# Block 0's first product, summed unit by unit in shared PSUM banks, with a new order of the whole program

## The chip, the cores and the metric

The kernel runs on one core of a Trainium2 chip. The metric is the device time of one execution in microseconds; the median of three runs of the kernel before is 976.9 us (976.35 to 977.07). A core has TensorE (PE, matrix products, with its weight loads PEld), VectorE (DVE), ScalarE (ACT), GpSimd (POOL) and SyncE (SP, which here only starts transfers). TensorE writes to PSUM, eight banks of 128 partitions x 512 fp32 values; VectorE and ScalarE read PSUM. Lines are quoted as L and a number; "before" and "now" numbers differ by up to 42, since the file grew.

## The reference

Random-feature attention, then a two-layer network on its output; the shapes are 8 batches, 8 heads, 576 positions, 64 columns, 128 features; 4608 tokens of width 512, hidden width 2048.

```python
def phi(x):                                  # x: q or k, scaled by 64 ** -0.25
    proj = einsum('bhsd,md->bhsm', x, omega)
    h = proj - sum(x * x, -1) / 2
    return exp(h - max(h, -1)) / sqrt(m)
kv = einsum('bhsm,bhsd->bhmd', k_p, v);  z = sum(k_p, axis=2)
num = einsum('bhsm,bhmd->bhsd', q_p, kv)
den = einsum('bhsm,bhm->bhs', q_p, z)[..., None] + 1e-06
x = (num / den).transpose(0, 2, 1, 3).reshape(4608, 512)
out = gelu(x @ w_in) @ w_out
```

The two weights arrive as 64-bit floats and are converted on the chip.

## The kernel before

**Work.** A *unit* is a pair of heads of one batch: 32 units, four to a batch (j = 0 to 3). The four units of a batch give the four 128-row slices of x, so a product x @ w_in over 512 columns is a sum of four pieces, one per unit. Units 0 to 7 are computed in plain fp32: projections (`pair`, L657, and `shared`, L664), maxima and shifts on VectorE (`top` L669, `shift_tiles` L678), exponentials on ScalarE (L673, L682), the sums over keys (`kv`, L689), transposes of q (`q_trans`, L727), numerators and denominators (`num_plain`, L737), reciprocals (`rcp`, L763 on) and the division into x (`div`, L800), each of the last in two halves. The later units use split numbers (`proj` L902, `proj_q` L924, `kv_split` L1003, `num` L746).

**Blocks.** The network runs over 13 blocks of tokens: 128, eleven times 384, 256. Block 0 uses the converted fp32 weights (`mm1` L1176, `gelu` L1187, `mm2` L1202). All others use weights and activations split in two fp16 parts, with three products for one: `mm1` (L1181) adds 12 products into a bank, `gelu` (L1189), `g_high` (L1193) and `g_low` (L1197) make the two parts, `mm2` adds three products (L1205 to L1207). The weights are converted in 16 pieces (`w_hi` L426, `w_lo` L435, `w_rmax` L438, `w_shift` L442, `w_round` L453), scaled by a maximum over all of them (`wchain_b` L503 and on), and then split (`w_high` L485 on ScalarE, `w_low` L489 on VectorE), 16 column blocks for each of w_in and w_out.

**Banks.** PSUM's eight banks form three rings: `at` with three buffers, `acc` with three, and `h` with two (`hb0`, `hb1`). The units of batch 0 may use all three rings, later units only `at`. Block 0's first product takes one `h` bank for each of 16 column blocks of 128.

**Order.** A planner (`Planner.run`) takes all operations with their costs and dependencies and lists them in time: on each engine it picks, among those that can start, the one with the earliest due time. Due times come from tables: `FIRST` gives a fixed sequence to the operations that it names, `STARTS` the blocks, `UDUE` the units' divisions, `OFF` a shift by kind of operation. The program is written in the order of that list, every engine runs its own part strictly in that order, and semaphores hold the dependencies. Where the planner sees TensorE without work, between `wk0` and `wk` microseconds of its own clock, it puts in `fill`: four products of the identity (L381) into columns of `hb0` that nobody reads.

## Time and profile before

| | |
|---|---|
| median of three runs | 976.9 us |
| profiled execution: device time | 975.53 us |
| its span, first to last instruction | 973.8 us |
| TensorE / weight loads busy | 963.4 / 602.3 us |
| VectorE / ScalarE / GpSimd busy | 715.4 / 730.0 / 350.4 us |
| identity products (L381) | 312, 21.8 us |
| block 0's first product (L1176) | 64 products, 17.4 us |
| granted TensorE clock | 1.00 |

A group row names line, engine, operation, tiles and shapes, the count, then busy time and the mean of one in ns (products overlap, so busy time over count is less than the mean), then idle time ahead of it and what ended that. An fp32 product leaves two records, an fp16, bf16 or rounded fp32 one leaves one. A timeline row has start, duration, engine, line, operation and count of equal instructions in a row; a bracket tells of idle time before it. The row of a stretch has busy time and instruction count of each engine, then granted clock, share of the transfer engines and GB/s.

### The profile page before, as it was taken

What the parts mean: (1) busy time and instruction counts of PE and PEld (TensorE: products, weight loads), DVE (VectorE), ACT (ScalarE), POOL (GpSimd) and SP (SyncE); (2) the same over time, 40 slices, a digit from 0 to 9 for tenths busy, and PEclk for the clock granted to TensorE, in tenths of its full rate; (3) what the DMA queues carried; (4) which work ended last, traced back from release to release, by engine and by line L of the source; (5) the groups of instructions that cost most, each with busy time, mean ns of one, the idle gap of its engine ahead of it and who ended that gap; (6) DMA issues with size and microseconds to landing.
All of it is one profiled execution on the core that took longest, in us unless ns stands there. A gap on an engine that the chain in (4) does not pass through costs nothing.

```text
span 973.8 us, 18152 instructions
## 1 busy us (share of the span) xinstructions
PE 963.4 (99%) x6324; PEld 602.3 (62%) x6324; DVE 715.4 (73%) x1948; ACT 730.0 (75%) x1504; POOL 350.4 (36%) x560
## 2 busy tenths in 40 slices
PE   8999999999999999999999999999999999999998
PEld 7777665665566666666565665566656656555576
DVE  5899899977888889878797888777767778621111
ACT  6979897887689879787798878877776986643243
POOL 2444334742166264353255335245216522200000
PEclk9999999999999999999999999999999999999999
DMA  8756123321041041031221132022003200000000
GB/s 305 229 182 227 70 73 134 98 82 55 1 118 61 26 139 47 25 91 45 75 82 49 30 127 66 14 72 61 24 33 86 62 23 12 1 33 1 1 34 22
DMA packets 39083, 70.96 MB, mean 73 GB/s; under 512 B 5712, under 2 KB 14288, under 8 KB 38992
## 3 DMA queue, kind: packets, MB, share of 16 engines
q1 hardware_dynamic: 38992, 69.81, 23.1%
q8 instruction: 50, 0.82, 0.4%
q14 instruction: 41, 0.34, 0.1%
HBM read 60.36 MB, written 9.44 MB: 72 GB/s over the span
## 4 chain that ended last, share of the span: by engine, by line
PE 96%; DVE 2%; DMA 1%; ACT 0%; issue 0%; SPq 0%; ACTq 0%; DVEq 0%
PE hb L1181 37%; PE acc L1205 12%; PE acc L1207 12%; PE acc L1206 12%; PE at L746 4%; PE at L924 3%; PE at L902 3%; PE at L1003 2%; PE hb L381 2%; PE hb L1176 2%; PE acc L1202 1%; PE at L657 1%; PE at L737 1%; PE at L689 1%; PE hb L689 1%; PE at L727 1%
## 5 line engine op out<-in xcount | busy, mean ns | idle before, releaser
L1181 PE MATMUL hb<-xh,wih 128*128 128x384 f16 (+1 forms) x768 | 247.2, 322 | 0.6 <-DVE gl L1197 0.4
L1181 PE MATMUL hb<-xl,wih 128*128 128x384 f16 (+1 forms) x768 | 247.2, 322 | 0.0
L1181 PE MATMUL hb<-xh,wil 128*128 128x384 f16 (+1 forms) x768 | 247.1, 322 | 0.0
L894 POOL TENSOR_TENSOR r<-xt,r 64x256 fp32r<-64x256 f32 (+2 forms) x216 | 171.8, 814 | 202.7 <-ACT r L889 161.3
L1205 PE MATMUL acc<-woh,gh 128*128 128x512 f16 (+1 forms) x560 | 211.4, 377 | 0.0
L1207 PE MATMUL acc<-wol,gh 128*128 128x512 f16 (+1 forms) x560 | 210.5, 376 | 0.0
L1206 PE MATMUL acc<-woh,gl 128*128 128x512 f16 (+1 forms) x560 | 210.5, 376 | 0.0
L1197 DVE SCALAR_TENSOR_TENSOR gl<-hb,bs,gh 128x384 f16<-128x384 f32 (+1 forms) x192 | 115.2, 600 | 126.0 <-ACT gh L1193 124.2
L1181 PEld LDWEIGHTS <-wih 128*128 128x128 f16 x1536 | 147.0, 98 | 95.2 <-issue 1.7
L1189 ACT ACTIVATE hb<-hb,bs 128x384 f32<-128x384 f32 (+1 forms) x192 | 104.5, 545 | 86.8 <-PE hb L1181 84.5
L1193 ACT ACTIVATE gh<-hb,bs 128x384 f16<-128x384 f32 (+1 forms) x192 | 109.2, 569 | 51.5 <-PE acc L1207 35.5
L1181 PEld LDWEIGHTS <-wil 128*128 128x128 f16 x768 | 75.1, 98 | 50.2 <-issue 1.6
L889 ACT CAST r<-xt 128x256 fp32r<-128x256 f32 (+2 forms) x216 | 81.5, 403 | 25.8 <-PE at L902 10.5
L1207 PEld LDWEIGHTS <-gh 128*128 128x128 f16 x576 | 56.4, 98 | 64.5
L1205 PEld LDWEIGHTS <-gh 128*128 128x128 f16 x576 | 56.1, 97 | 47.4 <-issue 0.4
L1206 PEld LDWEIGHTS <-gl 128*128 128x128 f16 x576 | 56.5, 98 | 42.1
L803 DVE TENSOR_TENSOR w<-at,rt 64x128 f32<-64x128 f32 (+6 forms) x168 | 54.7, 325 | 4.3 <-DVE rt L770 0.5
L757 ACT ACTIVATE dt<-at,vsc 64x288 f32<-64x288 f32 x96 | 47.6, 495 | 5.2 <-PE at L746 3.0
L902 PE MATMUL at<-om,r 128*128 128x256 f32 x216 | 50.3, 325 | 0.2
L924 PE MATMUL at<-r,om 128*128 128x288 f32 x192 | 50.4, 351 | 0.0
L906 ACT COPY lo<-at 128x256 f32<-128x256 f32 (+1 forms) x120 | 40.4, 349 | 2.2 <-PE at L902 1.5
L963 DVE TENSOR_TENSOR ql<-qt,qh 128x576 fp32r<-128x576 f32 x48 | 37.3, 782 | 6.1 <-ACT qh L960 6.0
(218 smaller groups left out, 1690.6 us busy)
## 6 DMA issues: line engine op xcount, KB each, us to landing
xt<-in_kT SPq DMA_DIRECT2D x56, 288.0 KB, 3.8
xt<-in_qT SPq DMA_DIRECT2D x56, 288.0 KB, 3.6
out_x<-o SPq DMA_DIRECT2D x35, 256.0 KB, 2.1
raw<-in_w_in SPq DMA_DIRECT2D x16, 512.0 KB, 5.2
raw<-in_w_out SPq DMA_DIRECT2D x16, 512.0 KB, 4.6
w<-in_v SPq DMA_DIRECT2D x6, 1280.0 KB, 6.1
wol<-in_v SPq DMA_DIRECT2D x6, 320.0 KB, 5.9
vt<-in_v SPq DMA_DIRECT2D x2, 320.0 KB, 4.1
```

Source lines behind the costliest of these rows:

```text
L803: nc.vector.tensor_tensor(x[r, c0:c1], ps[r, r0:r1], rt[r, r0:r1], op=ALU.mult)
L889: nc.scalar.copy(G['r', u, x][:, 0:b - a], xf[:, a:b])
L894: nc.gpsimd.tensor_tensor(r, xf[D:, a:b], r, op=ALU.subtract)
L902: nc.tensor.matmul(o[:, t], r[:, t * P:(t + 1) * P], om, start=True, stop=True)
L924: nc.tensor.matmul(G['pp', u, NK + g][:, 0:HS], om[:, i], xr_part(u, NK + g), start=(i == 0), stop=(i == 1))
L1181: nc.tensor.matmul(h[:, 0:t], w, (G['xh', n, j], G['xh', n, j], G['xl', n, j])[k][:, 0:t], start=(i == 0), stop=(i == 3 * NJ - 1))
L1189: nc.scalar.activation(h, h, AF.Gelu, scale=G['bs', n][:, 2:3])
L1193: nc.scalar.activation(G['gh', n, c][:, 0:t], G['h', n, c][:, 0:t], AF.Copy, scale=G['bs', n][:, 3:4])
L1197: nc.vector.scalar_tensor_tensor(G['gl', n, c][:, 0:t], G['h', n, c][:, 0:t], G['bs', n][:, 3:4], G['gh', n, c][:, 0:t], op0=ALU.mult, op1 ...
L1205: nc.tensor.matmul(acc, gh[:, s], woh[:, c, c0:c1], start=(c == 0), stop=False)
L1206: nc.tensor.matmul(acc, gl[:, s], woh[:, c, c0:c1], start=False, stop=False)
L1207: nc.tensor.matmul(acc, gh[:, s], wol[:, c, c0:c1], start=False, stop=(c == NF - 1))
```

## The change

Block 0's first product takes one `h` bank for three column blocks (`HG = 3`; columns 0 to 383 of the bank, side by side; the sixteenth block is alone in the sixth). Each of the 64 products is an operation of its own (`mm1_early`) that depends on its column block's weights and its unit's x alone, so the slice of unit 0 can be added before unit 1 is done. Only the first product into a bank carries the start flag. `gelu` reads its third of a bank once all twelve products of that bank are in. `fill` no longer carries the start flag, since sums may be open in the same bank. `fill` ends at 60 us of the planner's clock in place of 100. All tables of the planner are new. The code for `nd2` is there, but `nd2` is 0, so `den` and `rcp` are as before.

```diff
-X = dict(fb=793.51, fbp=-272.45, fb0=327.13, fbb=-89.81, ..., wk=100.0, wk0=5.0, nd=1, sr=0, pmx=0, m0=5)
+X = dict(fb=739.58, fbp=-521.51, fb0=-190.76, fbb=289.99, ..., wk=60.0, wk0=5.0, nd=1, sr=0, pmx=0, m0=5, nd2=0, e0=1)
-FIRST = (1, 3, 0, 2, 6, 7, 8, 40, 4, 5, 42, 110, 76, 144, 41, ...
+FIRST = (1, 3, 6, 7, 2, 0, 40, 41, 142, 151, 4, 157, 5, 8, 10, ...
...
+    HG = 3
...
     def fill():
         for i in range(4):
-            nc.tensor.matmul(hb[0][:, T:], iz[:, 0:P], iz[:, P:], start=True, stop=True)
+            nc.tensor.matmul(hb[0][:, T:], iz[:, 0:P], iz[:, P:], start=False, stop=True, skip_group_check=True)
...
+    def hcols(c):
+        return G['h', 0, c // HG * HG][:, c % HG * TB[0]:(c % HG + 1) * TB[0]]
+
+    def mm1_early(c, j):
+        nc.tensor.matmul(hcols(c), wi32[:, c, j], xs(0, j)[:, 0:TB[0]], start=(c % HG == 0 and j == 0), stop=(j == NJ - 1), skip_group_check=True)
+
     def gelu(n, c):
         t = TB[n]
+        if n < N32 and X['e0']:
+            nc.scalar.activation(G['g', n, c][:, 0:t], hcols(c), AF.Gelu)
+            return
...
         if n < N32:
             xr = [xs_place(n, j)[1] for j in range(NJ)]
+            if X['e0']:
+                if c % HG == 0:
+                    key = ('h', n, c)
+                    cs = range(c, min(c + HG, NF))
+                    for j in range(NJ):
+                        for x in cs:
+                            op('PE', t * 4 / 2400 + .02, mm1_early, x, j, r=[('w32', 1, x), xr[j]], w=[key] if (x, j) != (c, 0) else [],
+                               new=[] if (x, j) != (c, 0) else [('h', key)], due=when(n, x + j / 4), kind='P')
+                op('ACT', 0.1 + t / 1000, gelu, n, c, r=[('h', n, c // HG * HG)], new=[('g', ('g', n, c))], tab='g', kind=k)
+                return
```

Three places of the built order. First TensorE, where the first pieces of block 0's first product stand now (L1210); before, L1176 first stands behind the first maximum of the weights. The other rows are the attention of units 1 to 3: projections (L670, L677), transposes (L740), key sums (L702) and unit 1's first numerator (L750); `hb_84` and `hb_85` are the two `h` banks, `w_71` the converted weights.

```order
L670 MATMUL at<-om_66,xt 128x128
L670 MATMUL acc<-om_66,xt 128x128
L740 MATMUL acc<-ident,w_71 128x128 x4
L1210 MATMUL hb_84<-xa,w_71 128x128
L702 MATMUL acc<-vt_73,et 128x65 x8
L702 MATMUL acc<-vt_73,et 128x130
L1210 MATMUL hb_85<-xa,w_71 128x128
L740 MATMUL at<-ident,w_71 128x128 x5
L1210 MATMUL hb_84<-xa,w_71 128x128
L677 MATMUL at<-om_66,xt 64x128 x4
L670 MATMUL acc<-om_66,xt 128x128 x8
L750 MATMUL acc<-w_71 64x288 x2
```

Three of the 18 products that now stand ahead of the first maximum are among these rows; two more stand just ahead and one just behind. In the old order none stands there.

Then TensorE at the mark that the prediction uses, the second numerator of unit 4. Before (the first row is unit 4's first numerator, the last two are the first of 16 equal pairs of identity rows, and the second numerator, L737, comes right behind those):

```order
L737 MATMUL at<-qh,kvz 64x288 x4
L1176 MATMUL hb_85<-xa,w_71 128x128 x4
L1176 MATMUL hb_84<-xa,w_71 128x128 x4
L1202 MATMUL acc<-w_71,g 128x512
L1176 MATMUL hb_85<-xa,w_71 128x128 x4
L657 MATMUL at<-om_66,xt 128x128 x8
L1176 MATMUL hb_84<-xa,w_71 128x128 x4
L1202 MATMUL acc<-w_71,g 128x512
L381 LDWEIGHTS ident
L381 MATMUL hb_84<-ident 128x128
```

Now (the last row is the second numerator):

```order
L670 MATMUL at<-om_66,xt 128x128 x8
L677 MATMUL at<-om_66,xt 64x128 x4
L1210 MATMUL hb_85<-xa,w_71 128x128 x8
L750 MATMUL at<-qh,kvz 64x288 x4
L1234 MATMUL acc<-w_71,g 128x512 x2
L1210 MATMUL hb_85<-xa,w_71 128x128 x3
L670 MATMUL at<-om_66,xt 128x128 x8
L1210 MATMUL hb_85<-xa,w_71 128x128
L750 MATMUL at<-qh,kvz 64x288 x4
```

Before, 16 identities stand between the second product (L1202) and that numerator; now unit 5's projections (L670) and one product of block 0 (L1210) stand directly ahead of it, and the identities are gone.

Last ScalarE, at block 1's first two activations (L1189 and its rounding L1193; L1221 and L1225 now). L485 (L498 now) are the splits of w_in (`wih`) and w_out (`woh`). Before:

```order
L711 ACTIVATE zr<-kvz 128x2
L485 ACTIVATE wih<-w_71,wsc 128x4x128 x5
L1189 ACTIVATE hb_85<-hb_85,bs 128x384
L1193 ACTIVATE gh<-hb_85,bs 128x384
L1212 COPY o<-acc 128x512
L1189 ACTIVATE hb_84<-hb_84,bs 128x384
L1193 ACTIVATE gh<-hb_84,bs 128x384
L485 ACTIVATE woh<-w_71,wsc 128x512 x4
```

Now:

```order
L498 ACTIVATE wih<-w_71,wsc 128x4x128
L744 COPY qh<-at 128x512
L498 ACTIVATE woh<-w_71,wsc 128x512 x5
L1221 ACTIVATE hb_85<-hb_85,bs 128x384
L1225 ACTIVATE gh<-hb_85,bs 128x384
L498 ACTIVATE woh<-w_71,wsc 128x512 x6
L1221 ACTIVATE hb_84<-hb_84,bs 128x384
L1225 ACTIVATE gh<-hb_84,bs 128x384
```

Ahead of the second rounding stand eleven more splits now, all of w_out: five ahead of the first activation and six behind it.

## The prediction

> **What bounds the kernel now.** I read the page first: busy shares, the forty slices, the chain that ended last.

> ```profile
> PE 963.4 (99%) x6324; PEld 602.3 (62%) x6324; DVE 715.4 (73%) x1948; ACT 730.0 (75%) x1504; POOL 350.4 (36%) x560
> DVE  5899899977888889878797888777767778621111
> PEclk9999999999999999999999999999999999999999
> PE 96%; DVE 2%; DMA 1%; ACT 0%; issue 0%; SPq 0%; ACTq 0%; DVEq 0%
> ```

> TensorE is busy for 963.4 of 973.8 us, and 96% of the chain is TensorE. Without the identity products every product is needed, so time can only come from the 10.4 us in which TensorE idles and from the identity products. VectorE is at 7 to 9 tenths for three quarters of the span: not the bound on average, perhaps in a stage. Next the groups of TensorE by line, which show the products that the change touches.

> ```profile
> L381 PE MATMUL hb<-ident 128*128 128x128 bf16 x312 | 21.8, 219 | 2.0 <-DVE w L698 0.6 <-DVE nm L669 0.5 <-ACT g L1187 0.4
> L1176 PE MATMUL hb<-xa,w 128*128 128x128 f32 x128 | 17.4, 281 | 0.0
> ```

> The 312 identity products (L381) cost 21.8 us, 0.070 us each; nothing reads them. Block 0's first product is 64 products in two records each, 17.4 us, 0.27 us per product. Then busy time by stretches, all engines, and below it that of the identity products alone.

> ```profile
> 20.00:30.00 10.00, 8.90 (x113) 7.21 (x112) 6.88 (x18) 8.89 (x26) 5.98 (x5) 1.00 0.86 262
> 40.00:50.00 10.00, 10.00 (x116) 7.62 (x113) 9.69 (x25) 9.60 (x28) 3.87 (x4) 1.00 0.70 231
> 60.00:70.00 10.00, 8.91 (x97) 7.39 (x97) 9.15 (x24) 7.03 (x11) 4.29 (x2) 1.00 0.63 201
> 80.00:90.00 10.00, 10.00 (x67) 7.33 (x63) 9.33 (x17) 9.47 (x13) 3.70 (x2) 1.00 0.58 209
> 120.00:140.00 20.00, 20.00 (x144) 12.78 (x143) 18.77 (x43) 18.93 (x33) 5.28 (x9) 1.00 0.24 69
> 140.00:180.00 40.00, 39.91 (x232) 22.66 (x231) 37.71 (x116) 32.14 (x75) 21.30 (x38) 1.00 0.40 126
> 700.00:800.00 100.00, 100.00 (x606) 59.66 (x605) 74.93 (x220) 80.86 (x169) 43.03 (x77) 1.00 0.15 44
> ...
> 20.00:30.00 10.00, 3.67 (x48) 2.93 (x48) 1.00 0.86 262
> 40.00:50.00 10.00, 2.91 (x40) 2.40 (x40) 1.00 0.70 231
> 60.00:70.00 10.00, 2.83 (x40) 2.63 (x41) 1.00 0.63 201
> 90.00:110.00 20.00, 0.39 (x4) 0.31 (x4) 1.00 0.46 162
> ```

> The columns after the stretch are TensorE, its weight loads, VectorE, ScalarE, GpSimd. A full TensorE before 70 us is an illusion: three tenths are identity products. From 80 us on there is nearly none, and TensorE stays full until the last stores. VectorE is at 9.69 of 10 at 40 to 50 and at 18.77 of 20 at 120 to 140. So the first 80 us are set by VectorE (and ScalarE, 9.60 at 40 to 50), with TensorE waiting under a cover of identities; afterwards TensorE sets the end with VectorE close behind. The time of the whole is the useful TensorE work that gets done in the first part.

> **The change, part by part.** *Identities.* The built program has 228 in place of 312: 84 x 0.070 = 5.9 us less. That isn't a gain yet: where TensorE would have waited anyway, an identity costs nothing, and its absence leaves a bare wait. The last of them now stand ahead of the first maximum of the weights (L503; L516 now), so no wait behind it has a cover.

> *The early products.* Their number and shapes are the same: cost 0. What moves is their place: 18 of the 64 now run before that maximum, where there were none; they need only the units done so far and the converted weights. They go into time that identities covered, so they are free where they lie and are worth 0.27 us each later. What counts is how much remains at a place whose time another engine sets.

> *The mark.* I take the second numerator of unit 4 (L737; L750 now), since there the trace shows who sets the time.

> ```profile
> 75.85 1.16 PE L657 MATMUL at<-om,xt 64*128 64x128 f32 x16
> 76.94 1.16 PE L1176 MATMUL hb<-xa,w 128*128 128x128 f32 x8
> 77.93 1.02 PE L1202 MATMUL acc<-w,g 128*128 128x512 f32 x2
> 78.79 1.06 PE L381 MATMUL hb<-ident 128*128 128x128 bf16 x16
> 79.78 1.19 PE L737 MATMUL at<-qh,kvz 128*64 128x288 f32 x8
> ...
> 77.04 1.29 DVE L669 TENSOR_REDUCE nm<-at 128x4 f32<-128x512 f32 x2 [0.61 <-PE at L657]
> 78.24 1.28 DVE L678 TENSOR_TENSOR et<-at,nm 128x512 f32<-128x512 f32 x2
> ```

> Unit 4's numerator needs `at` banks that unit 5's projections hold until VectorE has shifted them (L678, ends at 79.52); TensorE fills with 16 identities and starts at 79.78. VectorE sets this time. I counted both orders up to the mark. Every kind of product stands there in the same number (96 projections, 45 products of keys and values, two of block 0's second product and so on), except two: 304 identities against 228, and 24 of block 0's first products against 36. So at the mark the changed kernel has 12 x 0.27 = **3.3 us** more useful work behind it. VectorE has, from the end of unit 3's first half (L800, 61.77) to the mark, the same instructions but for one more weight split (L489), and one small reduction (L500) less.

> ```profile
> 61.25 0.52 DVE L800 TENSOR_TENSOR xa<-hb,rt 128x128 f32<-128x128 f32 x2
> 61.69 0.15 DVE L500 TENSOR_REDUCE wcm<-wmax 128x1 f32<-128x8 f32 x1
> L489 DVE SCALAR_TENSOR_TENSOR wil<-w,wsc,wih 128x512 f16<-128x512 f32 x13 | 9.4, 745 | 0.0
> ```

> That is 0.745 - 0.15 = **0.6 us** later, if unit 3 is ready when it was. The gain at the mark is 3.3 - 0.6 = 2.7. Behind it the old order has eight more identities, 8 x 0.070 = **0.6 us**, and the new one none. Sum: -3.3 us; 5.9 us of identities go, 2.6 us come back as bare waits, mostly ahead of this mark.

> *Where unit 3 is ready.* I take the old time. Bounds from both sides: the new order does the shared projections (L664) of units 0 and 1 together at the start, which answers VectorE's longest early wait, 3.0 us; that is the most I give it. Against it, omega is loaded after two of the inputs instead of before them, 0.58 + 0.43 us of issue, so all may start 1.0 us later; yet TensorE's own first wait, 1.96 us for an input, can shrink by as much.

> ```profile
> DVE nm L669 <- PE acc L664: 3.0, 2, 2.6
> 2.00 0.58 SPq L642 DMA_DIRECT2D xt<-in_kT  x1
> 2.63 0.43 SPq L642 DMA_DIRECT2D xt<-in_qT  x1
> 8.66 0.37 PE L657 MATMUL at<-om,xt 64*128 64x128 f32 x1 [1.96 <-DMA xt<-in_kT]
> ```

> *After the mark.* The new order puts more weight splits ahead of block 1's first activations: 27 in place of 16 ahead of the second rounding (L1193; L1225 now). Their cover is ScalarE's waiting.

> ```profile
> 120.88 0.58 ACT L1193 ACTIVATE gh<-hb,bs 128x384 f16<-128x384 f32 x1
> 121.36 2.55 ACT L485 ACTIVATE woh<-w,wsc 128x512 f16<-128x512 f32 x4
> 121.49 0.62 DVE L1197 SCALAR_TENSOR_TENSOR gl<-hb,bs,gh 128x384 f16<-128x384 f32 x1 [0.18 <-ACT gh L1193]
> 123.85 0.33 PE L1181 MATMUL hb<-xh,wih 128*128 128x384 f16 x1
> ACT g L1187 <- PE hb L381: 2.2, 1, 2.2
> ACT hb L1189 <- PE hb L1181: 1.9, 2, 1.4
> ACT g L1187 <- PE hb L1176: 1.8, 4, 0.7
> ```

> Eleven splits at 2.55 / 4 = 0.64 are 7.0 us; between 60 and 121 us ScalarE waited 2.2 + 1.9 + 1.8 us for TensorE, which is now earlier, and some 1.2 in smaller waits. I take 0, as nearly all of it is covered; the other end is a rival below. It and the early 3.0 us stand on opposite sides, and I let them cancel. The later blocks, 140 us on, have the same products in another order; TensorE was full there and I take 0, with 0.5 us either way (of the 40 us from 140 it idled 0.09).

> *Sum.* The profiled execution: span 973.8 - 3.3 = 970.5. Its device time was 975.53, and the median of the three runs is 976.9; the same 3.3 off the median gives **973.6 us**.

> **Rivals.** (1) *The front is released too.* VectorE's early 3.0 us wait goes and nothing eats it later: 973.6 - 3.0 = 970.6. For it: VectorE has 6.88 of 10 at 20 to 30. Against: it is full from 40, and ScalarE has no room either.

> (2) *The waiting only loses its cover.* VectorE sets not just the mark but everything up to 140 us; TensorE, 3 us ahead, runs into it again and the lead goes in waits for banks: 976.9 - 0.6 = 976.3, no change. For it: VectorE at 94% from 120 to 180. Against: part of its own idle time there is waiting for TensorE.

> (3) *Block 1's activations come late* (slower). If ScalarE gets none of its waits back, the second rounding lands at 120.88 + 0.58 + 7.0 = 128.5, VectorE's rest (0.62) at 129.1, and only then is the bank free for block 1's fourth column block. TensorE came there at 123.85 and now would at 123.85 - 3.3 + 1.1 (eight projections stand ahead of it now) = 121.7. It waits 7.4 us: 973.6 + 7.4 = 981.0. It decides from the point where that rounding ends later than about 124; the 5.9 us of waits above speak against it.

> (4) *A bare wait slows the products behind it.* The warm-up shows a slow start: 22 products of 256 columns in 4.23 us, 0.192 each, where identities of 128 columns later follow at 3.08 / 52 = 0.059.

> ```profile
> 1.05 4.23 PE L377 MATMUL hb<-w 128*128 128x256 bf16 x22 [1.05 <-DVE w L368]
> 10.34 3.08 PE L381 MATMUL hb<-ident 128*128 128x128 bf16 x52
> ```

> At twice 0.059 the warm-up would take 2.6 us, so it lost 1.6. Should one bare wait after 60 us bring that state back, it costs 1.6 us and the wait: 973.6 + 1.6 = 975.2. Against: the longest wait in the trace, the 1.96 us above, was followed by no such thing. [...]

> **How the numbers follow.** Forecast 0.38; (1) 0.24; (2) 0.24; (3) 0.10; (4) 0.04. Two tenths of a per cent, 1.95 us, is about what a measurement here tells from no change: faster is under 974.9, slower over 978.9. The forecast and (1) are faster, 0.62; (2) and (4) are the same, 0.28; (3) is slower, 0.10. The forecast's own range is 972 to 975. The range for 8 in 10 is 968.8 to 977.6: it holds (1) with the start moved by 1 us and 0.5 us of the later blocks, and (2); it leaves out most of (3).

> **What would show it.** Right: identities near 16 us; 18 early products ahead of L516, without a wait; TensorE's useful work at unit 4's second numerator 3.3 us ahead, that numerator at 79.5 to 80.5; bare TensorE waits of 2 to 3 us between 60 and 85 us, for VectorE. Rival (1): the last division of unit 3's first half before 59.5. (2): several TensorE waits on `at` between 85 and 140, 3 us in sum. (3): a TensorE wait of several us for `hb` at 120 to 130, ended by VectorE's L1229 or ScalarE's L1225. (4): identities or products at twice their spacing after a wait. A front that is later than before, or TensorE waits after 180 us, would break the forecast in a way that none of these covers.

## The result and the profile after

The changed kernel takes 992.18 us (median of four runs, 986.56 to 993.59) against 976.62 for the kernel before: ratio 1.0151, 95% interval 1.0133 to 1.0169. It is 15.6 us slower; forecast were 3.3 us less, with a range that ended at 977.6. The profiled execution took 991.73 us, its span is 989.4. The runs of the changed kernel spread over 7 us, and the time goes with the mean granted clock: 0.998 at 986.56, 0.995 at 991.73, 0.992 at 992.63, 0.993 at 993.59. The four runs of before lie within 0.9; in the later rounds of 13 to 22 runs they span 2.4 to 5.7 us, the longest, 981.76, at a mean clock of 0.998.

The page of the changed kernel: busy shares, forty slices, the chain that ended last; then the group of the identities.

```profile
PE 969.2 (98%) x6240; PEld 602.1 (61%) x6240; DVE 721.3 (73%) x1948; ACT 729.0 (74%) x1504; POOL 360.6 (36%) x560
PEclk9989999999999999999999999999999999999999
PE 78%; DVE 7%; ACT 4%; POOL 4%; DMA 3%; issue 2%; SPq 1%; ACTq 0%; POOLq 0%; DVEq 0%
L394 PE MATMUL hb<-ident 128*128 128x128 bf16 x228 | 16.5, 237 | 0.0
```

Three differences stand here. TensorE is busy 5.8 us longer, although 84 identities are gone and no product was added. One digit of the granted clock is an 8. And TensorE holds 78% of the chain instead of 96%: VectorE, ScalarE, GpSimd and transfers now have places in it.

Where the time went can be read with equal work. I priced each product of TensorE at the median distance from its start to the next start of its kind in the kernel before (identities and warm-up at nothing) and looked up when a given amount of such work had been started. In the kernel before, 170 us of it have been started at 198.7 us; the front below is all up to there.

| against before, us | front | behind it | sum |
|---|---|---|---|
| changed kernel | +7.3 | +7.6 | +14.9 |
| e1, cover for two bare waits | +3.0 | +7.5 | +10.5 |
| e7, V first and cover | +1.2 | +6.3 | +7.5 |
| e8, as e7, old later order | +1.7 | +1.6 | +3.3 |
| e6, before with the new later order | -0.4 | +13.2 | +12.8 |

These are profiled executions, one each (e8's took 978.95 us, 1.3 over its median, e7's 984.13, 1.3 under, that of the kernel before 975.53, 1.4 under). So about half was lost ahead of 200 us and half behind it, where I had forecast no loss at all. The stretches of five us in the front (columns as in the prediction):

```profile
15.00:20.00 5.00, 2.59 (x32) 2.41 (x29) 3.23 (x5) 3.84 (x7) 0.85 (x2) 1.00 1.04 394
20.00:25.00 5.00, 5.00 (x51) 4.77 (x52) 1.22 (x5) 3.84 (x16) 5.00 (x4) 0.66 1.08 352
60.00:65.00 5.00, 2.89 (x24) 2.38 (x20) 4.90 (x9) 2.51 (x8) 1.59 (x1) 0.94 0.84 260
65.00:70.00 5.00, 5.00 (x33) 4.94 (x33) 4.04 (x14) 3.22 (x8) 2.23 (x1) 0.50 0.06 23
```

TensorE is idle for over 2 us in the first and the third, and in the stretch after each the granted clock is 0.66 and 0.50. The trace's records of the clock show two stretches at half while TensorE works, 3.41 us from 19.99 and 6.83 us from 64.37. If 10.24 us at half clock do the work of 5.12, 5.12 us are lost, an estimate from these lengths (the rows below show 1.8 and 1.9 times the time); part of that work is identities. TensorE at these places:

```profile
18.31 2.71 PE L702 MATMUL hb<-vt,et 128*128 128x65 f32 x18 [2.41 <-POOL vt L638]
20.81 3.42 PE L394 MATMUL hb<-ident 128*128 128x128 bf16 x36
...
31.39 1.29 PE L394 MATMUL hb<-ident 128*128 128x128 bf16 x20
36.18 2.17 PE L702 MATMUL acc<-vt,et 128*128 128x65 f32 x18
...
64.29 4.12 PE L702 MATMUL at<-vt,et 128*128 128x65 f32 x18 [2.11 <-ACT et L686]
68.21 2.34 PE L394 MATMUL hb<-ident 128*128 128x128 bf16 x20
```

Twenty identities take 1.29 us at 31 us and 2.34 at 68; the key sums (nine fp32 products, 18 records) take 2.17 us at 36 and 4.12 at 64. Both slow stretches follow a bare wait: 2.41 us for GpSimd's copy of unit 0's V (L638), 2.11 us for ScalarE's exponentials of unit 4 (L686).

The first has a plain cause. GpSimd's copies of V, first in the changed kernel, then in the one before:

```profile
17.54 0.72 POOL L638 COPY vt<-wol 128x640 f32<-128x640 f32 x1 [16.23 <-DMA wol<-in_v]
```

```profile
7.95 0.72 POOL L625 COPY vt<-wol 128x640 f32<-128x640 f32 x1 [6.65 <-DMA wol<-in_v]
```

Unit 0's V is ready 9.6 us later. SP's queue, first in the changed kernel, then in the one before:

```profile
3.99 0.43 SPq L635 DMA_DIRECT2D wol<-in_v  x1
4.46 3.11 SPq L435 DMA_DIRECT2D raw<-in_w_in  x4
7.62 5.20 SPq L635 DMA_DIRECT2D wol<-in_v  x5
```

```profile
3.10 0.43 SPq L622 DMA_DIRECT2D wol<-in_v  x1
...
7.91 3.44 SPq L422 DMA_DIRECT2D raw<-in_w_in  x4
```

In both a part of V is loaded ahead of the weights; but in the new order that one part is unit **4**'s. Unit 0's comes behind two pieces of the weights (four loads, L435). The rows show the tile, and all six parts go into one tile (`wol`), so the name does not tell them apart; the table `FIRST` does (142 is unit 4's load, 8 is unit 0's: "41, 142, 151, 4, 157, 5, 8").

The second has two parts: VectorE is late, and it stalls. VectorE, ScalarE and GpSimd ahead of the 2.11 us:

```profile
59.23 2.36 POOL L466 TENSOR_TENSOR w<-w 128x1024 int32<-128x1024 int32 x1 [1.86 <-ACT w L448]
60.42 1.20 DVE L777 TENSOR_SCALAR rc<-rt 128x9 f32<-128x9 f32 x1
62.31 1.25 DVE L682 TENSOR_REDUCE nm<-at 128x4 f32<-128x512 f32 x2
63.05 1.14 ACT L686 ACTIVATE et<-at,nm 128x128 f32<-128x128 f32 x4 [2.43 <-DVE nm L682]
...
65.53 0.17 DVE L777 TENSOR_SCALAR rc<-rt 128x9 f32<-128x9 f32 x1
```

Adding the small constant to nine denominators per row (L777) takes 0.17 us at 65.53; at 60.42 it takes 1.20 and ends with GpSimd's rounding, at 61.6. Only then come the maxima (L682) for which ScalarE's exponentials wait 2.43 us. How much of TensorE's wait is the stall's was not tried in the changed kernel.

Behind 180 us the waits of TensorE by what ended them (in total, times, longest) have one row in the kernel before, and these first ones in the changed kernel:

```profile
PE hb L1181 <- DVE gl L1197: 0.4, 1, 0.4
```

```profile
PE at L947 <- POOL r L917: 1.5, 3, 1.0
PE at L925 <- DVE w L823: 0.9, 1, 0.9
PE hb L1204 <- DVE gl L1229: 0.9, 3, 0.4
PE at L925 <- POOL r L917: 0.8, 2, 0.5
PE at L925 <- ACT gh L1225: 0.7, 1, 0.7
```

The projections of the later units (L925, L947) now stand where their inputs are not yet rounded or divided. The rows add up to 4.8 us.

### The profile page after: what moved, and what is told of

The parts are those of the page before. It is cut to its first block, busy times and chain, and to the rows that moved or that the text cites. A ratio compares the mean times of both kernels' runs of the same rounds, so it can differ in the third digit from the quotient of the medians.

```text
span 989.4 us, 17903 instructions
## 1 busy us (share of the span) xinstructions
PE 969.2 (98%) x6240; PEld 602.1 (61%) x6240; DVE 721.3 (73%) x1948; ACT 729.0 (74%) x1504; POOL 360.6 (36%) x560
## 4 chain that ended last, share of the span: by engine, by line
PE 78%; DVE 7%; ACT 4%; POOL 4%; DMA 3%; issue 2%; SPq 1%; ACTq 0%; POOLq 0%; DVEq 0%
PE hb L1204 32%; PE acc L1237 10%; PE acc L1239 10%; PE acc L1238 10%; PE at L759 3%; PE at L925 2%; PE at L1026 2%; PE at L947 2%; POOL r L917 1%; DMA wol<-in_v 1%; DMA w<-in_v 1%; DVE xl L1193 1%; DVE w L823 1%; POOL w L466 1%; PE at L750 1%
## 5 line engine op out<-in xcount | busy, mean ns | idle before, releaser
L917 POOL TENSOR_TENSOR r<-xt,r 64x256 fp32r<-64x256 f32 (+2 forms) x216 | 176.3, 833 | 214.8 <-ACT r L912 149.4
L1229 DVE SCALAR_TENSOR_TENSOR gl<-hb,bs,gh 128x384 f16<-128x384 f32 (+1 forms) x192 | 115.0, 600 | 128.6 <-ACT gh L1225 126.6
L1221 ACT ACTIVATE hb<-hb,bs 128x384 f32<-128x384 f32 (+1 forms) x192 | 104.3, 544 | 87.5 <-PE hb L1204 85.6
L1225 ACT ACTIVATE gh<-hb,bs 128x384 f16<-128x384 f32 (+1 forms) x192 | 109.2, 570 | 65.3 <-PE acc L1239 52.2
L947 PE MATMUL at<-r,om 128*128 128x288 f32 x192 | 50.0, 348 | 1.5 <-POOL r L917 1.5
L925 PE MATMUL at<-om,r 128*128 128x256 f32 x216 | 49.0, 324 | 2.4 <-DVE w L823 0.9
L365 POOL TENSOR_SCALAR w<-et 128x256 f16<-128x256 f32 (+1 forms) x65 | 24.3, 402 | 47.0 <-ACT et L695 41.8
L1026 PE MATMUL at<-vb,w 128*128 128x129 f16 (+3 forms) x432 | 41.0, 212 | 0.1
```

What stands on the lines that cost most here:

```text
L917: nc.gpsimd.tensor_tensor(r, xf[D:, a:b], r, op=ALU.subtract)
L925: nc.tensor.matmul(o[:, t], r[:, t * P:(t + 1) * P], om, start=True, stop=True)
L947: nc.tensor.matmul(G['pp', u, NK + g][:, 0:HS], om[:, i], xr_part(u, NK + g), start=(i == 0), stop=(i == 1))
L1221: nc.scalar.activation(h, h, AF.Gelu, scale=G['bs', n][:, 2:3])
L1225: nc.scalar.activation(G['gh', n, c][:, 0:t], G['h', n, c][:, 0:t], AF.Copy, scale=G['bs', n][:, 3:4])
L1229: nc.vector.scalar_tensor_tensor(G['gl', n, c][:, 0:t], G['h', n, c][:, 0:t], G['bs', n][:, 3:4], G['gh', n, c][:, 0:t], op0=ALU.mult, op1 ...
```

## The experiments

Each time is the median, in brackets lowest and highest and the number of runs; the ratio is to the kernel before on the same chip, with its 95% interval. The five rounds (e1 to e4, e5 to e8, e9 and e10, e11 and e12, e13 and e14) ran on five chips, and the median of the kernel before lies between 976.35 and 977.30 us in them; so a difference of under 1 us between two rounds says nothing.

### e1: cover for the two bare waits

```diff
+    COVER = {23: 10, 613: 9}     # key sums of unit 0, of unit 4
     def put(o):
+        for i in range(COVER.get(o.id, 0)):
+            put_fn(fill)
         put_fn(o.fn, *o.a)
```

> The changed kernel with 76 identity products more: 40 directly ahead of the first sums of keys and values of unit 0, where TensorE waited 2.41 us bare, and 36 directly ahead of those of unit 4, where it waited 2.11 us. Nothing else moves. Theory A (the bare waits let the granted clock fall to a half, 3.4 us after the first and 6.9 us after the second, and the work lost there is never made up): the granted clock is back at 1.00 in every slice, and the time is 984 to 987.5. Theory B (VectorE's lateness comes from the late load of V and from its own stalls; TensorE's clock hardly matters, since VectorE sets the time there): clock back at 1.00, but the time stays at 989 to 992.

987.29 us (986.94 to 987.61, 4); 1.0111 (1.0094 to 1.0127). The clock is full until TensorE's last products (means of 0.999 to 1.000), the long waits are gone, and the runs lie within 0.7 us instead of 7. 76 identities more make the kernel 4.9 us faster: theory A. The same numerator behind the second stretch, in the changed kernel and in e1:

```profile
70.48 1.52 PE L750 MATMUL acc<-w 128*64 128x288 f32 x8
```

```profile
66.38 1.19 PE L750 MATMUL acc<-w 128*64 128x288 f32 x8
```

Of the 4.6 us between these two executions 4.1 are won by then. 10.5 us stay.

### e2: unit 0's V ahead of the weights

```diff
-FIRST = (1, 3, 6, 7, 2, 0, 40, 41, 142, 151, 4, 157, 5, 8, 10, ...
+FIRST = (1, 3, 6, 7, 2, 0, 40, 41, 8, 151, 4, 157, 5, 142, 10, ...
```

> The changed kernel with two loads exchanged in the order of SP's queue: unit 0's part of V goes in the sixth place, where unit 4's stood, ahead of the first two pieces of the weights. The 40 identities ahead of unit 0's sums move behind them, as the planner now finds V there in time; else the same. Theory A (the late V is the first cause: it makes TensorE wait 2.41 us, brings the first stretch at half clock, and leaves VectorE about 3 us behind at 30 us): the sums of unit 0 start before 16.5 instead of at 18.31, VectorE's work done at 60 us is at least 2.5 us more than in the changed kernel, and the time is 985 to 988. Theory B (the loss is made in the later stages, 60 us and on, whatever the start): 990 to 993.

987.95 us (986.15 to 988.86, 4); 1.0115 (1.0100 to 1.0130): theory A, 4.2 us from the place of one load. V is copied at 8.75 and the key sums start at 13.42. VectorE's work done at 60 us, priced by the medians of before, is 3.2 us behind that kernel; in the changed kernel it was 5.3 behind. That is 2.1 us gained, a little less than the 2.5 expected. The second bare wait is still there (2.10 us), ahead of it a stall of the same addition (1.18 us instead of 0.17), and behind it the clock:

```profile
60.00:65.00 5.00, 4.09 (x28) 4.06 (x29) 4.84 (x17) 4.03 (x12) 0.61 (x1) 0.69 0.30 115
65.00:70.00 5.00, 5.00 (x34) 3.43 (x33) 2.07 (x5) 1.90 (x5) 1.90 (x2) 0.63 0.88 263
```

### e3: the kernel before, identities only to 60 us

```diff
-wk=100.0
+wk=60.0
```

> The kernel before with one number changed: identities stop at 60 us of the planner's time instead of 100, as in the change; nothing else of the change. Theory A (identities are needed as cover wherever TensorE waits): a wait of about 2 us now lies bare between 61 and 72 us, the granted clock falls below 1.00 there, and the time is 979 to 984. Theory B (what matters is one long bare wait in one stretch; the old order has no wait of 2 us there, and several short ones do no harm): clock 1.00 throughout and 975.5 to 977.5.

976.64 us (974.49 to 978.00, 10); 0.9998 (0.9988 to 1.0007): no change, theory B. Its longest bare wait behind 60 us is the one below, and the clock stays at 1.00 until the end. So it isn't the missing identities between 60 and 100 us as such; in the old order no wait of 2 us lay under them.

```profile
PE at L727 <- ACT et L682: 0.8, 1, 0.8
```

### e4: cover, and the old numbers for the later order

```diff
-STARTS, UDUE, OFF, fb, fbp, fb0, fbb: the change's
+STARTS, UDUE, OFF, fb, fbp, fb0, fbb: those of before
```

> As the changed kernel with the 76 identities more, and besides the later order by the old tables: the starting times of the blocks, the due times of the units, the offsets by function and the four bonuses are those of the kernel before, while the list of the first 997 operations, the change's, stays. TensorE's order is the same to about 200 us and then goes by the old tables. Theory A (the 6 to 7 us that the changed kernel loses after 400 us are made by its new later order): 4 to 7 us below the run with the 76 identities alone. Theory B (they follow from the late start): within 1.5 us of that run.

993.63 us (991.90 to 994.96, 4); 1.0174 (1.0158 to 1.0190): neither theory. It is 6.3 us slower than e1. The old numbers behind the new front give a third order, with a wait of 2.30 us at 508, 6.83 us of half clock behind it, and in that a second wait of 2.87 us. It shows how far such tables hang on the list in front of them, and nothing on the question; e5 and e6 take the order itself.

### e5 and e6: the later order itself, exchanged

```diff
-        for n, i in enumerate(FIRST):
+        for n, i in enumerate(FIRST + LATE):     # LATE: the other kernel's order of all operations not in FIRST
             self.ops[i].due = n - 1e6
```

> As e1_cover (the changed kernel with 76 identity products ahead of the two bare waits), and the operations behind the first 997 get the order in which the kernel before issues them, as a fixed list, in place of the change's order. e4 couldn't tell whether the late loss is the order's own, as the old numbers with the new front gave a third order; this gives the old order itself (TensorE's groups behind 205 us agree with it to 97.7%). Theory A (the 7 to 8 us between 200 us and the end are made by the new later order, whatever the start): 978.5 to 981.5, against 987.3 of e1_cover. Theory B (they follow from how the front ends): 986 to 989.

> The other way round: the kernel before, with its own first 752 operations (to about 160 us) and identities, and behind them the order in which the changed kernel issues the same operations (groups of TensorE behind 205 us agree with the changed kernel's to 87%). No part of the front changes. Theory A (the later order costs by itself): 981.5 to 986. Theory B (it doesn't): 975.5 to 978.5.

e5: 979.25 us (978.31 to 980.80, 10); 1.0019 (1.0006 to 1.0031), 8.0 us under e1. e6: 988.31 us (986.54 to 992.04, 4); 1.0110 (1.0076 to 1.0143), 11.3 us over before without any change in the front. Theory A both times, e6 by more than I had given it: behind the old front the new order meets other waits, among them one of 2.32 us at 580 with 3.41 us of half clock after it. Its waits behind 180 us:

```profile
PE hb L1390 <- DVE gl L1406: 4.8, 7, 2.3
PE at L1212 <- DVE w L1201: 3.8, 2, 2.4
PE at L1111 <- ACT gh L1402: 1.3, 1, 1.3
```

The later order costs by itself, 8 us behind the new front and 11 behind the old. How much is due to the places of which projection wasn't tried; in the changed kernel the waits named above are 4.8 of the 7.6 us, and most of the rest lies in TensorE's busy time, where ends of products are modelled.

### e7 and e8: V first and cover, without and with the old later order

> As e2_v_first (unit 0's part of V loaded ahead of the weights), and 36 identities more ahead of the sums of unit 4, where e2 still shows a bare wait of 2.10 us and behind it 6.8 us at half clock. Theory A (half clock costs time on the path): clock 1.00 throughout and 984 to 986.3, against 987.95. Theory B (VectorE sets the time there and TensorE's slow stretch is hidden): 987.3 to 989.

> All three together: V first, the 36 identities ahead of unit 4's sums, and the later order of the kernel before. If the three causes are separate and complete (late V, bare wait, later order), their gains add up and nothing of the loss is left: 976 to 978.5. If something else of the new front costs too (TensorE idles 3.7 us more than before between the first 40 and the first 80 us of its useful work): 978.5 to 981.

e7 (the exchange of e2, and `COVER = {613: 9}`): 985.38 us (984.13 to 986.36, 4); 1.0074 (1.0048 to 1.0100), clock 1.00 in all runs, 2.6 us under e2: theory A. e8 (and `LATE` of e5): 977.67 us (977.02 to 980.85, 10); 1.0009 (0.9994 to 1.0023). So late V and bare waits are worth 6.8 us together (4.2 and 4.9 alone: the first wait is in both; with the waits covered, V's place is worth 1.9 us from e1 to e7 and 1.6 from e5 to e8, neither clear of noise), the later order 7.7, and what is left of the change is no difference that can be told. In e7 unit 4's second numerator comes in two halves, the second where I had put the whole, the first 1.7 us ahead of that:

```profile
77.84 0.71 PE L750 MATMUL at<-qh,kvz 128*64 128x288 f32 x4
79.56 0.71 PE L750 MATMUL at<-qh,kvz 128*64 128x288 f32 x4 [1.01 <-DVE et L691]
```

At 80 us e7 has 3.5 us and e8 3.2 us more useful work started than the kernel before. At 115 us they are 0.9 and 1.1 us behind it: between 80 and 115 us TensorE idles 3.1 us in both, and 0.0 in the kernel before. The next runs ask what makes it wait.

### e9 and e10: another form of the stalling addition

```diff
-            nc.vector.tensor_scalar(rc, rv[:, :, 0], EPS, None, op0=ALU.add)
+            nc.vector.tensor_tensor(rc, rv[:, :, 0], epst, op=ALU.add)      # epst: a tile filled with EPS
```

> The kernel before with one operation of VectorE in another form: the addition of the small constant to nine columns of denominators (L764, one input and an immediate) reads the constant from a tile instead (two inputs). In the profile of before 4 of 16 of these took 0.8 us on the mean instead of 0.17, 2.5 us in all, each ending as GpSimd's rounding of a weight piece (2.36 us) ended. Theory A (the one-input form must wait for GpSimd, the two-input form needn't; VectorE sets the time in the front): none of the 16 takes over 0.4 us, and the time is 974.8 to 976.4, 0.5 to 2 us under before. Theory B (they wait for something that both forms need): the long ones stay, and the time is that of before, within 0.5 us.

> e8 (unit 0's V first, cover ahead of unit 4's sums, the old later order) with the same other form. There 6 of 16 were long, 5.0 us in all, of them 3.0 us before 62 us. Theory A (these stalls are what holds VectorE, and by it TensorE, back between 40 and 90 us, where the forecast's lead of 3.3 us is lost): 974 to 976.3. Theory B (VectorE's other work sets it, or the stalls only move): 977 to 978.5.

e9: 976.70 us (975.06 to 980.62, 12); 1.0003 (0.9993 to 1.0014). e10: 978.34 us (977.22 to 980.45, 10); 1.0015 (1.0005 to 1.0026). Theory B: the stalls stay as long in the new form. In e9 one of them and the group of 16:

```profile
64.11 1.24 DVE L766 TENSOR_TENSOR rc<-rt,epst 128x9 f32<-128x9 f32 x1
L766 DVE TENSOR_TENSOR rc<-rt,epst 128x9 f32<-128x9 f32 x16 | 5.2, 326 | 0.6
```

My idea of the cause was too narrow: the traces show both forms held up, the one with two inputs, which took 1.24 us at 64.11 in e9, and the one with one input, which took 1.24 us at 64.14 in the kernel before, each 0.17 at its shortest. In the changed kernel all four additions that started well inside a rounding of a weight (L466, 2.4 us) took 0.6 to 1.6 us more than 0.17, and they ended within 0.04 us of it. Four maxima (L682, 0.68 to 0.69 us), six transposes (L776, 0.47 to 0.48) and a reciprocal (L727, 0.15) that started beside the same roundings took what they take elsewhere (medians 0.68, 0.47 and 0.16). Why the additions alone of these are held isn't shown.

### e11 and e12: without the addition

```diff
-            nc.vector.tensor_scalar(rc, rv[:, :, 0], EPS, None, op0=ALU.add)
-            nc.vector.reciprocal(rc, rc)
+            nc.vector.reciprocal(rc, rv[:, :, 0])
```

> e8 without the addition of the small constant to the denominators of the first eight units (the reciprocal reads the transposed sums directly): 16 operations of VectorE less, 7.4 us with their stalls behind GpSimd, 5.0 us of it stall. This part of the computation is left out. Reciprocals that fell beside GpSimd's roundings showed no stall in the changed kernel or before. Theory A (the stalls hold VectorE, and so TensorE, back between 40 and 90 us): the reciprocals stay at 0.2 us, and the time is 973.5 to 976, against 977.7. Theory B (VectorE's other work sets it): 977 to 978.3.

> The kernel before without the same additions (this part of the computation is left out): 16 operations of VectorE less, 5.3 us with 2.5 us of stalls. If VectorE's time in the front is worth its full length at the end: 971.5 to 973. If only the part of it ahead of about 85 us that nothing else hides counts: 974 to 976. If VectorE's time there is worth nothing, since other engines set the front of this order: 976.2 to 977.2.

e11: 977.42 us (976.34 to 979.38, 11); 1.0008 (0.9999 to 1.0017): theory B. e12: 976.10 us (974.98 to 977.34, 11); 0.9992 (0.9983 to 1.0001), 1.2 us under a median of before of 977.3 and not clear of noise; of the three answers on record the second and the last, that VectorE's time there is worth nothing, each miss by 0.1 us, so e12 decides nothing between them. Taking 7.4 us from VectorE left TensorE's waits of e8 between 60 and 140 us as they were. e8, then e11:

```profile
PE acc L1432 <- POOL w L664: 1.8, 3, 1.3
PE at L948 <- DVE et L889: 1.0, 1, 1.0
PE at L720 <- DVE ct L717: 0.9, 1, 0.9
```

```profile
PE acc L1431 <- POOL w L664: 1.8, 3, 1.3
PE at L948 <- DVE et L889: 1.0, 1, 1.0
PE at L720 <- DVE ct L717: 0.6, 1, 0.6
```

So VectorE is 98% busy at 70 to 90 us in e8, and yet 7.4 us less of it do not move this front.

### e14 and e13: less of GpSimd's roundings, then less of ScalarE

```diff
-        nc.gpsimd.tensor_tensor(pc.b, pc.b, pc.l or raw(pc)[1], op=ALU.add)
+        nc.gpsimd.tensor_tensor(pc.b[:, 0:512], pc.b[:, 0:512], (pc.l or raw(pc)[1])[:, 0:512], op=ALU.add)
 # e13 besides:
-        nc.scalar.activation(pc.l or raw(pc)[1], raw(pc)[1].bitcast(U32), AF.Copy, scale=2.0 ** -29)
+        nc.scalar.activation((pc.l or raw(pc)[1])[:, 0:512], raw(pc)[1][:, 0:512].bitcast(U32), AF.Copy, scale=2.0 ** -29)
```

> e8 with GpSimd's rounding of the weight pieces on half their columns only (the other half of the weights stays without its low part: this part of the computation is left out): 16 operations of 2.36 us become about 1.2. Theory A (the new front loses its lead of 3 us between 80 and 115 us since TensorE waits for roundings, and GpSimd's own time makes them late): the waits of block 0's second product for the rounding (0.3 and 1.3 us at 74 and 83 us) go, and the time is 974.5 to 976.5, against 977.7 of e8. Theory B (the roundings are late because ScalarE hands the pieces on late): each ends 1.2 us earlier and the waits shrink by that at most, but TensorE meets the next one; 976.5 to 978.

> As e14, and ScalarE's conversion of the low words on half their columns as well (left out with the same half): 16 operations of ScalarE of 1.15 us become about 0.6, some 9 us less of ScalarE between 10 and 110 us. Theory A (ScalarE, 9 to 10 tenths busy from 70 to 110 us, sets the pace there): 1.5 to 3 us below e14. Theory B (it doesn't; the pace is set by the loads of the weights or by the order itself): within 0.8 us of e14.

e14: 976.42 us (974.62 to 980.15, 10); 0.9995 (0.9981 to 1.0009). e13: 973.50 us (972.92 to 974.44, 6); 0.9966 (0.9951 to 0.9981). The first is 1.3 us under e8, at the edge between the two ranges, but 0.7 of that is the difference between the medians of the kernel before on the two chips, and the intervals of the two ratios overlap, so its time shows nothing. Its waits do: those for the roundings go, which was theory A, but others come in their place (1.2 us for exponentials), which was B. The second is 2.9 us below the first, in the same round: theory A. Their waits between 60 and 140 us, e14 and then e13:

```profile
PE at L949 <- DVE et L890: 1.3, 1, 1.3
PE at L901 <- ACT et L894: 1.2, 2, 1.0
```

```profile
PE at L950 <- DVE et L891: 1.3, 1, 1.3
PE acc L1434 <- ACT g L1415: 0.5, 1, 0.5
```

Some 9 us of ScalarE (an estimate: half of 16 operations of 1.15 us) are worth 2.9 us at the end, where 7.4 us of VectorE were worth nothing that can be told from noise. That fits ScalarE as the engine that sets the pace in this front, but does not show it alone: ScalarE's cut was made with the roundings halved and VectorE's with them whole, and e13 also gets each weight piece ready sooner. VectorE's cut on top of e14, and ScalarE's without e14, were not tried, nor either in the old front.

## Why the prediction was wrong

**What bounds the kernel.** That the first 80 us are set by VectorE was read from busy shares. e11 speaks against it for the new front, and e13 points at ScalarE, which I had listed beside VectorE with 9.60 of 10 and then dropped. A full engine is not yet the one on which the others wait.

**The identities and the early products.** Right as counted: 228 identities, 16.5 us, and 18 early products ahead of the first maximum. That missing identities cost nothing by themselves was right for the old order, e3; in the new one two long waits lay bare.

**The mark.** The forecast had unit 4's second numerator at 79.5 to 80.5 with 3.3 us more useful work behind it. In the changed kernel its halves start at 84.61 and 86.32, and TensorE is 1.3 us *behind* at 80. With V first and the cover (e7) they start at 77.84 and 79.56, and the lead is 3.5 us. So the lead at the mark was sized rightly, once its footing is put back. That it lasts to the end, the step "After the mark" with its sum of 0, failed: by 115 us the lead is gone (e7, e8).

**"Where unit 3 is ready. I take the old time."** This step failed first. I looked at the start for omega and the inputs, 1.0 us either way, and did not see that unit 0's V had gone behind the weights, since the six loads of V carry one tile name. The place of one load cost 4.2 us (e2), part of it by way of the first bare wait. My note that a later front would break the forecast "in a way that none of these covers" came true; a range for it I didn't give.

**The bare waits.** I had named rival (4), a bare wait that brings the slow state back, with 0.04 and 1.6 us. It happened twice, 10.24 us at half clock, and cover for the two waits was worth 4.9 us (e1). I held against it that 1.96 us of waiting had done no harm. That was one case, and I let it stand for all; the last section shows how it lay on the grid of the clock's changes. Also, I expected bare waits of 2 to 3 us in sum, and did not ask whether they would come in one piece.

**"The later blocks ... I take 0, with 0.5 us either way."** The second large failure: 7.7 us (e7 to e8). I had grounds to see that all tables were new, and judged a stretch of 834 us by the fact that the old order kept TensorE full there. That fact belonged to the old order.

**The rivals.** (1), the front released, is the opposite of what came. (2), the lead that runs into waits, is what e7 and e8 show behind 80 us: 3.2 to 3.5 us of lead at 80 are gone at 115. Its size came true, 3.1 us of waits there, but not its cause: they are not waits on `at` for VectorE alone, and the longest, 1.3 us, is on `acc` for GpSimd's rounding of a weight. With the rest undone the change is worth nothing that can be told, 977.67 against 977.05. (3), a late second rounding of block 1, did not come: no wait of TensorE for `hb` by VectorE's L1229 or ScalarE's L1225 is among those between 60 and 180 us. The side on which the result lies, slower by more than 0.2%, had 0.10, all of it on (3).

**What adds up.** Of 15.6 us, 6.8 are the late V and the two bare waits (to e7), 7.7 the later order (to e8), and 0.6 is left, inside the noise of e8 against before (-0.6 to +2.2 us); the last 0.4 is the difference between the medians of the kernel before in the two rounds. The 3.3 us of the forecast are the lead that did not last.

## What to carry to other kernels

Where a change brings a new order of the whole program, price every stretch of it: a row that names only the tile hides which part is loaded, and a stretch that kept an engine full did so in its own order. When idle-time filler goes, ask how long the longest single bare wait will be, not how long all waits are together (here the clock's falls came behind single waits of 2.1 to 2.4 us; e3, with none over 0.8 us behind 60 us, had no fall). And busy shares do not say which engine sets the pace: take time from one engine at a time, each from the same base, and see whether the waits move.

## What the runs showed of the hardware

The records of the clock in the changed kernel's trace start at 6.34 us and have changes at 19.99, 23.41, 64.37, 71.19 and, behind the last product, 989.38 us: 4, 5, 17, 19 and 288 times 3.413 us after that start. In the kernel before they start at 4.48 us and have one change, behind the last product, at 973.86: 284 times 3.413 us later. So in both traces every change lies on a grid of 3.413 us. Cut along it, the stretches ahead of the changed kernel's two falls, from 16.58 and from 60.95 us, hold 1.73 and 2.11 us of TensorE's waiting, a half and three fifths of them; no other stretch from 6.34 us to its last product holds more than 1.30. Where a wait lies on the grid may thus matter beside its length, and times of one program could differ from run to run by it, as those of the changed kernel do (986.56 to 993.59 us). That this is the reason isn't shown, as one execution of each is profiled.

The same grid, laid over the other traces from their own records of the clock, sorts the waits. The stretches ahead of all five falls held 1.7 to 2.3 us of waiting. The waits without a fall were split between two stretches: 1.19 and 0.77 us in the kernel before, 1.41 and 0.70 in e12, 1.02 and 1.40 in e6. No stretch with 1.55 us or less was followed by a fall. An exact limit does not come out of this: behind the last products of e8 a stretch with 1.80 us was not followed by one.

Small additions of VectorE (0.17 us alone) that met an operation of GpSimd took up to 1.73 us in the changed kernel: five of 16, 4.6 us too long in all, four beside roundings of weights (L466) and one, at 136.84, beside L917. In the kernel before four of 16 were 2.5 us too long in all, three beside roundings of weights (L453) and one, at 150.76, beside L920. Without the additions, and so without 5.0 us of stalls in e8 and 2.5 in the kernel before, the time did not change by more than the noise (e11, e12).
